# A third of some softmax tiles exponentiated on VectorE, unpadded projections, and a paced background queue

## The chip, the cores and the metric

The kernel runs on one core of a Trainium2 chip. The metric is device time in microseconds (us) of one execution. The engines are named as in the profile: PE (matrix multiply), ACT (activation functions), DVE (vector), POOL (GpSimd) and SP (here only an issuer of DMAs). [...]

## The reference

One transformer block on a sequence of 2048 rows of 512 features, 32 heads of 16, all inputs in bf16:

```python
def _A_ref(x, wqkv, wo):                       # attention
    qkv = (x @ wqkv).reshape(B, S, 3, H, Dh)   # transposed to q, k, v: [B, H, S, 16]
    scores = einsum("bhqd,bhkd->bhqk", q, k) * (Dh ** -0.5)
    o = einsum("bhqk,bhkd->bhqd", softmax(scores), v)
    return o.reshape(B, S, D) @ wo
def _B_ref(x, w_gate, w_up, w_down):           # feed-forward, F = 1792
    return (sigmoid(x @ w_gate) * (x @ w_up)) @ w_down
h  = x + _A_ref(layernorm(x), wqkv, wo)
h2 = h + _B_ref(layernorm(h), w_gate, w_up, w_down)
```

The 32 heads times 2048 times 2048 scores make 134 million exponentials; on 128 partitions that is 2048 blocks of 128 x 512.

## The kernel before

The program has three stages.

**The prologue** (lines 78 to 235) loads x and the weights, normalises x in four chunks of 512 rows (`chunk_ln`), transposes it on PE into `xnT`, projects K and Q of the first four heads and all of V (`v_tile`, 16 tiles of 128 rows), and finds a bound for the softmax shift: the largest squared norm of a key (`kmax_mm`, `kmax_red`, `kmax_fin`) and of each query (`q_shift`). The shift is written as a 17th row beside the 16 rows of Q, against a row of ones beside K, so that the score matmul subtracts it. Heads sit at 32-row steps: the projection weights are copied into zero-padded tiles (`wk_pad`, `wq_pad`), so one projection matmul gives 4 heads in 128 columns of which 64 are used. `wo_pad` is padded in the same way.

**The loop** (lines 462 to 486) goes over 683 tiles. A tile is three blocks (the last has two): a block is 128 keys of one head against 512 queries. The order is query chunk `qc` (4), head group `g` (8 of four heads), key tile `kt` (16), head `j` (4). For each tile PE makes three score matmuls into one of two PSUM tiles `pss` (L403; the four heads use four 32-row strips of the array), ACT exponentiates all 1536 columns in one instruction into `pt` (L471), and PE multiplies by V with a column of ones into `acc` (L431; 17 columns at four 32-column strips). PE's program order is: scores of tile n+1, then `av(...)` for three or six blocks of earlier tiles, then one `step()` of the background queue.

The background queue `bg` holds Python generators that issue everything else a piece at a time: K and Q projections of the other head groups (`prep_k`, `prep_q`), and, for a finished chunk, the output projection and LayerNorm (`wo_ln`) and the feed-forward (`ffn`). Each `yield` ends a tile's share: mostly four matmuls of 128 x 128 x 512, in every tile that has them. All of it goes through one PSUM bank `pm`, which DVE or ACT must read before the next piece may write. When a group's 16 key tiles are done, `finish_group` transposes and divides `acc` on DVE.

**The tail** (lines 488 to 513) does output projection, LayerNorm and feed-forward of the last chunk, with nothing beside it.

Names for the steps: `pss` scores, `pt` exponentials, `acc` sums, `pm` background bank, `th` tanh, `hT` gated product, `sh` the shift row, `kr` and `k` the key maxima.

Of the kernel before, what the change touches and what calls it, by code (L numbers as in the profile page):

```python
# [10 lines left out]
BF16 = mybir.dt.bfloat16  # L11
I32 = mybir.dt.int32
# [3 lines left out]
ENG = mybir.EngineType  # L16


@with_exitstack
def kernel(  # L20
# [18 lines left out]
    NG = H // 4  # L39
    FC = F // P  # L40
# [4 lines left out]
    VW = DH + 1  # L45
    PSUM = bass.MemoryType.PSUM
# [45 lines left out]
    nc.gpsimd.memset(Vaug[:, :, :, DH:DH + 1], 1.0)
    nc.gpsimd.memset(wo_pad[:], 0.0)
    nc.vector.memset(sel[:], 0.0)
    for j in range(4):
        nc.vector.memset(sel[32 * j:32 * j + DH, j:j + 1], 1.0)
    nc.vector.tensor_reduce(out=e16[:], in_=ident_bf[:, DH:P:32], axis=AX.X, op=ALU.add)
    for b in o2buf:
        nc.vector.memset(b[:], 0.0)
    wo_v = A_wo.rearrange("(g j r) n -> j r g n", j=4, r=DH)  # L100
    for j in range(4):
        nc.gpsimd.dma_start(out=wo_pad[32 * j:32 * j + DH, :, :], in_=wo_v[j])
# [4 lines left out]
    def bank0():  # L107
        return ps0.tile([P, 512], FP32, name="b0")

    def ln_stats(src, mv):  # L110
        st = small.tile([P, nc.vector.BN_STATS_DIM], FP32, name="st")
        nc.vector.bn_stats(out=st[:], in_=src)
        nc.vector.bn_aggr(out=mv, in_=st[:])

    def ln_apply(dst, src, mv, rstd):
        nc.vector.tensor_scalar(out=dst, in0=src, scalar1=mv[:, 0:1], scalar2=rstd,  # L116
                                op0=ALU.subtract, op1=ALU.mult)

    def transpose4(ps, src):
        pt = ps[:].bitcast(BF16)[:, 0:DC * P].rearrange("p (b q) -> p b q", b=DC)  # L120
# [362 lines left out]
    while avq:  # L483
        av(GU)
# [59 lines left out]
```

## Time and profile before

| | us |
|---|---|
| median of 6 runs (1169.43 to 1174.78) | 1171.15 |
| the profiled execution, its own time | 1169.7 |
| its span from first to last instruction | 1167.9 |
| first exponential starts | 72.93 |
| last accumulation after the exponentials starts | 1109.60 |

Busy over the span: ACT 84%, PE 80%, DVE 23%, POOL 7%. Busy shares are means over stages: the stretches with background matmuls and those without behave differently, and the granted clock of PE differs between them. In the rows, a time in front is the start or the stretch in us from the span's start; `<-` behind an idle time names what ended it.

### The profile page before, as it was taken

What the parts mean: (1) busy time and instruction counts of PE and PEld (TensorE: products, weight loads), DVE (VectorE), ACT (ScalarE), POOL (GpSimd) and SP (SyncE); (2) the same over time, 40 slices, a digit from 0 to 9 for tenths busy, and PEclk for the clock granted to TensorE, in tenths of its full rate; (3) what the DMA queues carried; (4) which work ended last, traced back from release to release, by engine and by line L of the source; (5) the groups of instructions that cost most, each with busy time, mean ns of one, the idle gap of its engine ahead of it and who ended that gap; (6) DMA issues with size and microseconds to landing.
All of it is one profiled execution on the core that took longest, in us unless ns stands there. A gap on an engine that the chain in (4) does not pass through costs nothing.

```text
span 1167.9 us, 13140 instructions
## 1 busy us (share of the span) xinstructions
PE 937.8 (80%) x5336; PEld 287.6 (25%) x5408; DVE 265.2 (23%) x526; ACT 980.5 (84%) x774; POOL 86.1 (7%) x82
## 2 busy tenths in 40 slices
PE   3668777877887888787787898788788888888878
PEld 1212222222222322222222232222222322222233
DVE  5423323311123211111123212211124211000063
ACT  2359899899987997999987997899988998999911
POOL 6022222200000000000000000100000000000000
PEclk9778899776577998756678999765678998555589
DMA  5000000050000000000000000000000001000000
GB/s 144 1 1 1 1 1 1 1 190 1 1 19 1 1 1 19 2 1 1 1 19 1 1 1 19 1 1 1 1 19 1 1 1 37 1 1 1 1 1 19
DMA packets 11741, 14.87 MB, mean 13 GB/s; under 512 B 928, under 2 KB 10528, under 8 KB 11680
## 3 DMA queue, kind: packets, MB, share of 16 engines
q1 hardware_dynamic: 9904, 11.93, 3.1%
q10 hardware_dynamic: 1584, 1.57, 0.4%
q0 software_dynamic: 192, 0.52, 0.3%
q8 instruction: 42, 0.69, 0.2%
q14 instruction: 19, 0.16, 0.0%
HBM read 11.80 MB, written 2.10 MB: 12 GB/s over the span
## 4 chain that ended last, share of the span: by engine, by line
ACT 39%; PE 32%; issue 16%; DVE 10%; DMA 1%; POOL 0%; SPq 0%; ACTq 0%; DVEq 0%; POOLq 0%
ACT pt L471 37%; PE pm L147 6%; PE pss L403 6%; PE acc L431 5%; PE pm L352 4%; PE pss L502 2%; DVE hT L347 2%; PE pm L309 2%; PE b L201 2%; ACT th L340 1%; DVE xn L116 1%; PE pm L336 1%; DVE KT L156 1%; PE pss L511 1%; PE pm L344 1%
## 5 line engine op out<-in xcount | busy, mean ns | idle before, releaser
L471 ACT ACTIVATE pt<-pss 128x1536 bf16<-128x1536 f32 (+1 forms) x683 | 941.5, 1553 | 83.9 <-PE pss L403 61.6
L403 PE MATMUL pss<-qt,KT 32*128 32x512 bf16 x2048 | 336.8, 481 | 131.0 <-ACT pt L471 119.7
L431 PE MATMUL acc<-pt,Vaug 128*17 128x512 bf16 x2048 | 340.2, 482 | 1.5 <-DVE xs L412 1.0
L403 PEld LDWEIGHTS <-KT 32*128 32x128 bf16 x2048 | 107.2, 94 | 410.5 <-issue 398.0
L431 PEld LDWEIGHTS <-Vaug 128*17 128x17 bf16 x2048 | 66.2, 89 | 222.6 <-issue 222.4
L412 DVE STREAM_TRANSPOSE xs<-acc 128x512 f32<-128x512 f32 x32 | 22.9, 717 | 430.3 <-PE acc L431 429.8
L161 POOL TENSOR_TENSOR sq<-qt 128x512 bf16<-128x512 bf16 x32 | 33.3, 1040 | 678.3 <-DVE qt L187 667.2
L347 DVE SCALAR_TENSOR_TENSOR hT<-th,pm 128x512 bf16<-128x512 f32 x42 | 28.8, 685 | 138.8 <-ACT pt L471 105.1
L336 PE MATMUL pm<-hnT,wg 128*128 128x512 bf16 x147 | 44.2, 395 | 12.6 <-DVE hT L347 10.8
L352 PE MATMUL pm<-wd,hT 128*128 128x512 bf16 x159 | 45.7, 397 | 10.6 <-DVE ob L362 8.6
L147 PE MATMUL pm<-xnT,wq_pad 128*128 128x512 bf16 x102 | 46.2, 543 | 4.8 <-issue 4.2
L344 PE MATMUL pm<-hnT,wu 128*128 128x512 bf16 x168 | 44.2, 386 | 0.0
L161 POOL TENSOR_TENSOR sq<-KT 128x512 bf16<-128x512 bf16 x32 | 33.3, 1041 | 98.8 <-DVE KT L156 57.5
L340 ACT ACTIVATE th<-pm 128x512 f32<-128x512 f32 x42 | 32.4, 773 | 9.3 <-PE pm L336 9.3
L195 DVE TENSOR_SCALAR sh<-pm,kmax 4x512 bf16<-4x512 f32 x31 | 22.9, 739 | 67.5 <-PE acc L431 36.1
L505 ACT ACTIVATE th<-pss 128x512 f32<-128x512 f32 x14 | 8.4, 598 | 35.1 <-PE pss L502 33.9
L147 PE MATMUL pm<-xnT,wk_pad 128*128 128x512 bf16 x105 | 31.6, 415 | 7.1 <-DVE KT L156 6.3
L156 DVE TENSOR_SCALAR KT<-pm,e 128x512 bf16<-128x512 f32 x28 | 21.0, 749 | 38.3 <-PE pm L147 38.3
L309 PE MATMUL pm<-wo_pad,ot 128*128 128x512 bf16 x90 | 25.6, 394 | 4.9 <-DVE h L314 3.6
L122 PE MATMUL b<-ident_bf,xn 128*128 128x128 bf16 x64 | 7.2, 254 | 25.4 <-DVE xn L116 25.4
L187 DVE CAST qt<-pm 128x512 bf16<-128x512 f32 x31 | 20.8, 672 | 24.2 <-PE pm L147 24.2
L336 PEld LDWEIGHTS <-wg 128*128 128x128 bf16 x168 | 15.4, 99 | 32.0 <-issue 22.9
(84 smaller groups left out, 401.6 us busy)
## 6 DMA issues: line engine op xcount, KB each, us to landing
xb<-in_A_x_dram SPq DMA_DIRECT2D x4, 512.0 KB
xr<-in_A_x_dram SPq DMA_DIRECT2D x4, 512.0 KB
out_dram<-ob SPq DMA_DIRECT2D x16, 128.0 KB
wg<-in_B_w_gate_dram SPq DMA_DIRECT2D x1, 1792.0 KB
wu<-in_B_w_up_dram SPq DMA_DIRECT2D x1, 1792.0 KB
wd<-in_B_w_down_dram SPq DMA_DIRECT2D x1, 1792.0 KB
wk_raw<-in_A_wqkv_dram ACTq DMA_DIRECT2D x1, 512.0 KB
wv_sb<-in_A_wqkv_dram ACTq DMA_DIRECT2D x1, 512.0 KB
```

Of the source, the lines that this page charges most:

```text
L147: nc.tensor.matmul(ps[:], lhsT=w_pad[:, d, 4 * g:4 * g + 4, :].rearrange("p h r -> p (h r)"), rhs=xnT[:, d, c * QC:(c + 1) * QC], start=(d ...
L156: nc.vector.tensor_scalar(out=dst, in0=ps[:], scalar1=e16[:, 0:1], scalar2=None, op0=ALU.add)
L161: nc.gpsimd.tensor_tensor(out=sq[:], in0=src, in1=src, op=ALU.mult)
L309: nc.tensor.matmul(ps[:], lhsT=OT[qc, g][:, i * P:(i + 1) * P], rhs=wo_pad[:, g, :], start=(g == 0), stop=(g == NG - 1))
L336: nc.tensor.matmul(ps[:], lhsT=wg[:, d, f * P:(f + 1) * P], rhs=hnT[:, d, :], start=(d == 0), stop=(d == DC - 1))
L340: nc.scalar.activation(out=th[:], in_=ps[:], func=ACT.Tanh, scale=0.5)
L344: nc.tensor.matmul(ps[:], lhsT=wu[:, d, f * P:(f + 1) * P], rhs=hnT[:, d, :], start=(d == 0), stop=(d == DC - 1))
L347: nc.vector.scalar_tensor_tensor(out=hT[:, f, :], in0=th[:], scalar=1.0, in1=ps[:], op0=ALU.add, op1=ALU.mult)
L352: nc.tensor.matmul(ps[:], lhsT=hT[:, f, i * P:(i + 1) * P], rhs=wd[:, f, :], start=(f == 0), stop=(f == FC - 1))
L403: nc.tensor.matmul(pss[:, ui, :], lhsT=KT[g][32 * j:32 * j + 32, kt * P:(kt + 1) * P], rhs=QT[qc, g][32 * j:32 * j + 32, :], start=True, s ...
L431: nc.tensor.matmul(state["acc"][32 * j:32 * j + VW, :], lhsT=Vaug[:, kt, 4 * g + j, :], rhs=pt[:, ui, :], start=(kt == 0), stop=(kt == NT ...
L471: nc.scalar.activation(out=pt[:, 0:w, :], in_=pss[:, 0:w, :], func=ACT.Exp, scale=DH ** -0.5)
```

## The change

It rewrites most of the kernel, with the same mathematics.

1. **Exponentials on DVE.** In 158 of the 683 tiles (counted in the program; about one in four) ACT exponentiates two of the three blocks, and DVE the third, by seven instructions: it scales the score to an integer whose high bits are the exponent of 2 and low 9 bits the fraction, and adds a quadratic correction (`dexp_first`). The program picks the tiles with two counters of planned time, `clock["A"]` for ACT and `clock["D"]` for DVE.
2. **Unpadded projections.** One projection matmul now covers 8 heads (`proj8`); DVE or ACT copies the result to SBUF and eight DMAs of 16 x 512 on SP's queue spread it to the 32-row steps (`spread`). K takes 16 projections in place of 32, Q 16 in place of 32; the output projection takes 4 matmuls per row tile in place of 8. Squares move from POOL to DVE. The shift row goes out on POOL's queue in place of SP's, as do the four small DMAs of `kr`.
3. **Pacing.** V sums are issued in even tiles, up to 8 at a time; background matmuls in odd tiles, at most 4; results are read out at the earliest one tile later.
4. **Prologue and tail.** Eight of the 16 V tiles move into the loop; statistics of chunk c+1 are issued ahead of the transposes of chunk c; normalising moves from DVE to POOL and ACT; POOL fills `QT` and `KT` of groups 4 to 7 in between; the key maxima stay on their partitions (no DMA in the prologue). In the tail, three of the four output projection matmuls of each row tile stand ahead of the last V sums.

The core of the diff:

```diff
-        nc.scalar.activation(out=pt[:, 0:w, :], in_=pss[:, 0:w, :], func=ACT.Exp,
-                             scale=DH ** -0.5)
-        av(GU if len(avq) <= 2 * GU else 2 * GU)
-        for ui, u in enumerate(group):
-            avq.append((u, pt, ui))
-        step()
+        pend = sum(c[0] for c in chain)
+        split = (w == GU and last_kt < NT - 4 and not chain
+                 and clock["D"] + pend <= clock["A"] + 0)
+        wa = w - 1 if split else w
+        eins = nc.scalar.activation(out=pt[:, 0:wa, :], in_=pss[:, 0:wa, :], func=ACT.Exp, scale=SC)
+        clock["A"] += 98 + 427 * wa
+        if split:
+            jins = dexp_first(pss[:, GU - 1, :], uns[-1])
+            tc.declare_no_dep(jins.ins, eins.ins, reason="two readers of different banks")
+        avq.extend(uns)
+        run_chain(clock["A"] - 400)
+        if n % 2 == 0:
+            av(8)
+            run_bg(0)
+        else:
+            run_bg(4)
+        run_chain(clock["A"] + 600)
+        clock["D"] = max(clock["D"], clock["A"] - 600)
...
+    def dexp_first(src, un):
+        J = dvx.tile([P, QC], U16, name="J", bufs=2)
+        dv(720)
+        jins = nc.vector.tensor_scalar(out=J[:], in0=src, scalar1=512 * SC * LOG2E, scalar2=512 * 127.0,
+                                op0=ALU.mult, op1=ALU.add)
...
+        chain.extend([
+            (210, lambda: V.tensor_scalar(out=a[:], in0=J[:], scalar1=511, scalar2=None,
+                                          op0=ALU.bitwise_and)),
+            (320, lambda: V.tensor_scalar(out=b[:], in0=J[:], scalar1=0xFE00, scalar2=None,
+                                          op0=ALU.bitwise_or)),
+            (460, lambda: V.tensor_tensor(out=b[:].bitcast(BF16), in0=a[:],
+                                          in1=b[:].bitcast(I16), op=ALU.mult)),
+            (330, lambda: V.tensor_scalar(out=a[:].bitcast(BF16), in0=a[:],
...
+            (460, lambda: V.tensor_tensor(out=a[:].bitcast(BF16), in0=a[:].bitcast(BF16),
+                                          in1=b[:].bitcast(BF16), op=ALU.mult)),
+            (690, lambda: V.scalar_tensor_tensor(out=r[:], in0=J[:], scalar=0.25,
...
+    def run_chain(limit):
+        while chain and clock["D"] < limit:
+            ns, f = chain.popleft()
+            dv(ns)
+            f()
...
+    def spread(dst_pair, src, cols):
+        for a in range(2):
+            for j in range(4):
+                r = (4 * a + j) * DH
+                nc.sync.dma_start(out=dst_pair[a][32 * j:32 * j + DH, cols], in_=src[r:r + DH, :])
...
-        nc.sync.dma_start(out=QT[qc, g][DH:P:32, :], in_=sh[:])
+        for a in range(2):
+            nc.gpsimd.dma_start(out=QT[2 * p + a][DH:P:32, :], in_=sh[4 * a:4 * a + 4, :])
...
+    c_stats(0)
+    xns = c_apply(0)
+    for c in range(NQC):
+        if c + 1 < NQC:
+            c_stats(c + 1)
+        c_trans(c, xns)
+        if c + 1 < NQC:
+            xns = c_apply(c + 1)
+        if c == 0:
+            fill(range(4, NG))
...
+        c_proj(c)
...
+    wide = [ps_s.tile([P, GU, QC], FP32, name="pss") for _ in range(2)]
+    hps = [wide[i % 2][:, i // 2, :] for i in range(TQ)]
+    for i in range(TQ):
+        wo_mm(hps[i], qc, i, 0, NP - 1)
     while avq:
-        av(GU)
+        st["n"] += 1
+        av(64)
```

How this moves the instructions, at three places. First PE in the feed-forward (matmuls only, `wg` and `wu` are the gate and up weights). Before:

```order
L403 MATMUL pss_4999<-qt_3802,KT1_81 128x512
L431 MATMUL acc_507<-pt_4973,Vaug_88 17x512
...
L431 MATMUL acc_507<-pt_4988,Vaug_88 17x512
L336 MATMUL pm_5010<-hnT_4776,wg_1994 128x512
...
L403 MATMUL pss_5015<-qt_3802,KT1_81 128x512
...
L431 MATMUL acc_507<-pt_5003,Vaug_88 17x512
L403 MATMUL pss_5026<-qt_3802,KT1_81 128x512
...
L431 MATMUL acc_507<-pt_5019,Vaug_88 17x512
L344 MATMUL pm_5035<-hnT_4776,wu_1996 128x512
```

Now, in the first feed-forward (`xnT0` is reused for the transposed input, `dr` holds a block that DVE made):

```order
L532 MATMUL pss_3765<-QT2_93,KT2_85 128x512
...
L584 MATMUL acc_528<-dr_3729,Vaug_99 17x512
L584 MATMUL acc_528<-pt_3742,Vaug_99 17x512
...
L584 MATMUL acc_528<-pt_3758,Vaug_99 17x512
...
L532 MATMUL pss_3787<-QT2_93,KT2_85 128x512
...
L422 MATMUL pm_3794<-xnT0_79,wg_1708 128x512
...
L532 MATMUL pss_3801<-QT2_93,KT2_85 128x512
```

Three V sums stood between the scores of every two tiles; now seven stand in one gap and the four gate matmuls alone in the next. The gate and up pieces were three tiles' worth for one of the 14 columns of F; they are now four.

Second, DVE late in the last chunk, where nothing of the background is left. Before, these rows are the end of one chunk's output and two finished groups:

```order
L420 STREAM_TRANSPOSE ot_7700<-o2_0_99 128x512
L362 SCALAR_TENSOR_TENSOR ob_7702<-pm_7646,h_6835 128x512
...
L362 SCALAR_TENSOR_TENSOR ob_7864<-pm_7813,h_6835 128x512
L412 STREAM_TRANSPOSE xs_7955<-acc_507 128x512
L414 RECIPROCAL rec_7957<-xs_7955 128x16
L417 TENSOR_TENSOR o2_1_100<-xs_7955,rec_7957 128x16x16
```

Now, behind a finished group there (one whole block of exponentials, `J` to `dr`, and the start of the next):

```order
L549 STREAM_TRANSPOSE xs_10081<-acc_528 128x512
L551 RECIPROCAL rec_10083<-xs_10081 128x16
L554 TENSOR_TENSOR o2_1_107<-xs_10081,rec_10083 128x16x16
L595 TENSOR_SCALAR J_10112<-pss_10092 128x512
L603 TENSOR_SCALAR da_10114<-J_10112 128x512
L605 TENSOR_SCALAR db_10115<-J_10112 128x512
L607 TENSOR_TENSOR db_10115<-da_10114,db_10115 128x512
L609 TENSOR_SCALAR da_10114<-da_10114 128x512
L613 TENSOR_TENSOR da_10114<-da_10114,db_10115 128x512
L615 SCALAR_TENSOR_TENSOR dr_10116<-J_10112,da_10114 128x512
L595 TENSOR_SCALAR J_10146<-pss_10134 128x512
```

DVE had four instructions per group there; it now has seven more for each split tile, back to back.

Third, PE at the end of the loop (`ot` are the finished groups of the last chunk). Before:

```order
L431 MATMUL acc_507<-pt_8718,Vaug_88 17x512
...
L431 MATMUL acc_507<-pt_8723,Vaug_88 17x512
...
L309 MATMUL pss_8744<-wo_pad_90,ot_7127 128x512
L309 MATMUL pss_8744<-wo_pad_90,ot_7415 128x512
...
L309 MATMUL pss_8744<-wo_pad_90,ot_8737 128x512
```

Now:

```order
L584 MATMUL acc_528<-pt_10297,Vaug_99 17x512
L368 MATMUL pss_10307<-wo_sb_101,ot_8653 128x512
L368 MATMUL pss_10307<-wo_sb_101,ot_9277 128x512
L368 MATMUL pss_10307<-wo_sb_101,ot_9824 128x512
L368 MATMUL pss_10308<-wo_sb_101,ot_8653 128x512
...
L584 MATMUL acc_528<-pt_10299,Vaug_99 17x512
...
L368 MATMUL pss_10307<-wo_sb_101,ot_10332 128x512
```

Twelve output projection matmuls now stand between the last scores' sums and the last two V sums.

## Rows read from the trace of the kernel before

**Rows 1.** The page, part 1: busy us of each engine, share, instructions.
```profile
PE 937.8 (80%) x5336; PEld 287.6 (25%) x5408; DVE 265.2 (23%) x526; ACT 980.5 (84%) x774; POOL 86.1 (7%) x82
```
**Rows 2.** L471 by stretch: stretch, its us, ACT busy (instructions), granted clock, DMA share, GB/s.
```profile
72.00:240.00 168.00, 147.93 (x108) 0.88 0.00 1
240.00:337.00 97.00, 93.08 (x70) 0.61 0.16 58
337.00:477.00 140.00, 120.42 (x86) 0.93 0.03 8
...
866.00:985.00 119.00, 104.46 (x74) 0.96 0.03 9
```
**Rows 3.** Stretches, all engines: PE, PEld, DVE, ACT, POOL busy; then as above.
```profile
985.00:1110.00 125.00, 105.94 (x559) 27.36 (x556) 8.43 (x16) 124.53 (x93) 0.00 (x0) 0.52 0.02 6
72.00:1110.00 1038.00, 855.24 (x4974) 251.15 (x5039) 208.65 (x394) 951.61 (x725) 61.38 (x59) 0.76 0.03 10
```
**Rows 4.** By line and shape, 985 to 1110: count | busy us, mean ns | idle.
```profile
L471 ACT ACTIVATE pt<-pss 128x1536 bf16<-128x1536 f32 x92 | 124.0, 1610 | 0.0
```
**Rows 5.** The same for the whole span: busy us, mean ns, idle before, releasers.
```profile
L471 ACT ACTIVATE pt<-pss 128x1536 bf16<-128x1536 f32 x682 | 940.6, 1554 | 83.9 <-PE pss L403 61.6 <-PE acc L431 22.1
L347 DVE SCALAR_TENSOR_TENSOR hT<-th,pm 128x512 bf16<-128x512 f32 x42 | 28.8, 685 | 138.8 <-ACT pt L471 105.1 <-PE pm L344 33.8
L156 DVE TENSOR_SCALAR KT<-pm,e 128x512 bf16<-128x512 f32 x28 | 21.0, 749 | 38.3 <-PE pm L147 38.3
L505 ACT ACTIVATE th<-pss 128x512 f32<-128x512 f32 x14 | 8.4, 598 | 35.1 <-PE pss L502 33.9 <-remote 1.1
```
**Rows 6.** Timeline (start, us, engine, line), first background matmuls, lower clock.
```profile
76.14 1.89 PE L147 MATMUL pm<-xnT,wk_pad 128*128 128x512 bf16 x4
...
80.33 1.45 ACT L471 ACTIVATE pt<-pss 128x1536 bf16<-128x1536 f32 x1 [0.47 <-PE pss L403]
```
**Rows 7.** One line: ns min/median/max, first and last start, form.
```profile
L116 DVE TENSOR_SCALAR xn<-xb,mv,rstd x16: 394/405/4307, 9.7 to 54.1; 128x512 bf16<-128x512 bf16 x16
```
**Rows 8.** Timeline in the first feed-forward, upper clock.
```profile
400.69 1.04 PE L344 MATMUL pm<-hnT,wu 128*128 128x512 bf16 x4
...
401.88 0.39 PE L403 MATMUL pss<-qt,KT 32*128 32x512 bf16 x3 [0.15 <-ACT pt L471]
...
402.20 0.39 PE L431 MATMUL acc<-pt,Vaug 128*17 128x512 bf16 x3
...
405.04 0.60 PE L431 MATMUL acc<-pt,Vaug 128*17 128x512 bf16 x6
```
**Rows 9.** Timeline in the last chunk, lower clock.
```profile
1041.40 0.61 PE L403 MATMUL pss<-qt,KT 32*128 32x512 bf16 x3 [0.20 <-ACT pt L471]
1041.95 0.60 PE L431 MATMUL acc<-pt,Vaug 128*17 128x512 bf16 x3
```
**Rows 10.** Timeline of the prologue.
```profile
9.66 4.31 DVE L116 TENSOR_SCALAR xn<-xb,mv,rstd 128x512 bf16<-128x512 bf16 x1
10.01 3.81 POOL L93 MEMSET wo_pad<- 128x4096 bf16 x1
...
33.61 5.32 PE L201 MATMUL b<-wv_sb,xnT 128*128 128x512 bf16 x16
...
65.53 2.63 SPq L174 DMA_DIRECT2D k<-kr  x4
...
69.33 0.14 DVE L178 TENSOR_REDUCE kmax<-k 4x1 f32<-4x4 f32 x1 [3.83 <-DMA k<-kr]
...
72.28 1.03 PE L403 MATMUL pss<-qt,KT 32*128 32x512 bf16 x6 [7.50 <-DMA qt<-sh]
72.93 4.24 ACT L471 ACTIVATE pt<-pss 128x1536 bf16<-128x1536 f32 x3 [8.18 <-PE pss L403]
```
**Rows 11.** DMA issues by line, median us from issue to landing.
```profile
wo_pad<-in_A_wo_dram POOLq DMA_DIRECT2D x4, 128.0 KB, 4.2
```
**Rows 12.** Timeline at the end of the loop.
```profile
1109.60 0.60 PE L431 MATMUL acc<-pt,Vaug 128*17 128x512 bf16 x2 [0.31 <-ACT pt L471]
```

More of the change, by code (lines that the diff above doesn't have):

```diff
@@ L39 @@
     NG = H // 4
+    NP = NG // 2
     FC = F // P
@@ L97 @@
[L97 to L102, printed above, removed]
-    ps0ctx = ExitStack()
-    ps0 = ps0ctx.enter_context(tc.tile_pool(name="ps0", bufs=8, space=PSUM))
-    def bank0():
-        return ps0.tile([P, 512], FP32, name="b0")
+    nc.vector.memset(sel[:], 0.0)
@@ new lines, in c_trans, with c_proj @@
+    def c_trans(c, xns):
+        for i in range(TQ):
+            pt = transpose4(bank0(), xns[i])
+            dst = xnT[c][:, :, i * P:(i + 1) * P]
+            if i % 2:
+                nc.scalar.copy(out=dst, in_=pt)
+            else:
+                nc.vector.tensor_copy(out=dst, in_=pt)
+    def c_proj(c):
+        pk = bank0()
+        proj8(pk, wk_sb, 0, c)
+        kd = work.tile([P, QC], BF16, name="kd", bufs=4)
+        nc.scalar.copy(out=kd[:], in_=pk)
+        spread(KT[0:2], kd, slice(c * QC, (c + 1) * QC))
+        sq = square(kd)
@@ new lines @@
+    xns = c_apply(0)
[7 more added lines that the diff above has]
+            fill(range(4, NG))
+        if c == NQC - 1:
+            pq = bank0()
+            nc.tensor.matmul(pq[0:8, :], lhsT=sel[:, 0:8], rhs=cst["sqq"][:], start=True, stop=True)
+            nc.scalar.activation(out=small.tile([P, 1], FP32, name="warm")[:], in_=eps_t[:],
+                                 func=ACT.Exp)
+        c_proj(c)
@@ L235 @@
+    k_fin(k4, 0)
+    q_shift(pq, 0)
+    for a in range(2):
+        for j in range(4):
+            r = 32 * j + DH * a
+            nc.gpsimd.dma_start(out=wo_sb[r:r + DH, :, :], in_=wo_v[a, j])
     ps0ctx.close()
@@ L393, with scores @@
     units = [(qc, g, kt, j) for qc in range(NQC) for g in range(NG)
              for kt in range(NT) for j in range(4)]
-    groups = [units[i:i + GU] for i in range(0, len(units), GU)]
-    state = {"acc": acc_init, "n2": 0, "qc_open": 0}
-    avq = deque()
-    def scores(group):
+    tiles = [units[i:i + GU] for i in range(0, len(units), GU)]
+    def scores(tl):
         pss = ps_s.tile([P, GU, QC], FP32, name="pss")
-        for ui, (qc, g, kt, j) in enumerate(group):
-            force(("q", qc, g))
+        for ui, (qc, g, kt, j) in enumerate(tl):
+            force(("q", qc, g // 2))
@@ new lines, in av @@
+    def av(limit):
+        if st["defer"]:
+            st["defer"] = False
+        i = 0
+        while i < len(avq) and limit:
+            un = avq[i]
+            qc, g, kt, j = un.u
+            if qc * NG + g != st["cur"]:
+                return
+            if un.ready is None or un.ready >= st["n"]:
+                i += 1
+                continue
+            force(("v", kt))
+            avq.pop(i)
+            limit -= 1
+            c = count.get((qc, g, j), 0)
+            count[qc, g, j] = c + 1
+            nc.tensor.matmul(acc[32 * j:32 * j + VW, :], lhsT=Vaug[:, kt, 4 * g + j, :],
+                             rhs=un.ap, start=(c == 0), stop=(c == NT - 1),
```

619 lines of the change are left out of this document (358 added, 261 removed).

## The prediction

> **What bounds the kernel now.** Read the page first [rows 1]: ACT is busy 84% of the span and PE 80%, so neither bounds all of it. Then the table by stage [rows 2, 3], which separates two kinds of stretch in the loop. Without background matmuls (four stretches, 469 us, 338 exponentials; the first and the last stand in the rows) PE is granted 0.52 to 0.61 of its clock and ACT hardly waits: in the last one it is busy 124.53 of 125 us, PE 105.94 [rows 3]. There, 92 instructions in 124.0 us [rows 4] make 1.348 us a tile; that is ACT's own pace. With background matmuls (the feed-forward, three stretches, 401 us, 244 exponentials; and the K and Q projections, 168 us, 108 exponentials) the grant is 0.88 to 0.96 and ACT waits. Last, the groups of the whole span [rows 5] say for whom: 83.9 us of idle time ahead of the exponentials, 61.6 of it ended by the score matmuls.
>
> So the loop, from the first exponential at 72.93 [rows 10] to the last V sums at 1109.60 [rows 12], 1036.7 us, is ACT's work plus waits. Its work is 683 x 1.348 = 921 us and 42 tanh: one alone takes 0.598 [rows 5], and some 0.1 of that hides behind a neighbour, as 1.45 alone [rows 6] against 1.348 in a row shows for the large one; 42 x 0.5 = 21. Together 942; 95 us are lost. By stage, stretch less exponentials x 1.348 less tanh: 168 - 146 = 22 in the projections, 401 - 329 - 21 = 51 in the feed-forward, 469 - 456 = 13 in the rest; the borders of the stages are the remainder.
>
> **The change, part by part.**
>
> *ACT's work.* 512 columns cost (1.45 - 0.598) / 2 = 0.426 us. 158 tiles lose one block: 158 x 0.426 = 67 us. New work: 942 - 67 = 875 us.
>
> *DVE's new work.* Seven instructions a split tile, none of which stands in the trace. The first reads PSUM: 0.749 as L156; the last has three operands: 0.685 as L347 [rows 5]. Three have one SBUF input: 0.405 is the median of L116 [rows 7], the upper bound; half of it, 0.20, is my lower one. Two have two SBUF inputs: between 0.41 and 0.69, the same two rows. The sum is 2.85 to 4.05 us. The program plans 3.19; since its 720 and 690 ns for the first and the last lie within 5% of the rows, I take 3.3. 158 x 3.3 = 521 us beside about 200 us that DVE has in the loop already (208.65 [rows 3]; fewer transposes, more squares): 721 of some 940 us. Even the upper end, 840, is covered by ACT's own time, so DVE's total is no limit; lateness of single results can be (a rival).
>
> *PE in the loop.* Every two tiles have two score groups, one batch of about six V sums and, where there is background, four matmuls. At the upper clock: scores 0.32 (401.88 to 402.20), six sums 0.60, four matmuls 0.96 of their 1.04 before the next group starts [rows 8]: 2 x 0.32 + 0.60 + 0.96 = 2.2 us. At the lower: scores 0.55 (1041.40 to 1041.95 [rows 9]), four matmuls 1.82 of their 1.89 [rows 6], so 0.45 each; six sums are two rounds of that and a hand-over, 1.0: 3.9 us. ACT needs 2 x 1.348, less 0.426 in about every second pair, plus half a tanh in the feed-forward: 2.74 us. PE is under it at the upper clock and over it at the lower. Before, a tile with a gate piece had 0.32 + 0.32 + 0.96 = 1.6 us against 1.348, so PE was late there even at the upper clock; paced, it isn't.
>
> *What stays lost.* By the program's order 68 tiles stand beside projections, 312 beside the feed-forward and its LayerNorm, 303 beside neither. Projections: 0.2 us a tile as before, 14 us. Feed-forward: a mean grant of 0.93 is the lower clock for a seventh of the time; in some 16 of 156 pairs PE takes 3.9 and not 2.74, 18 us, and 7 for hand-overs. Rest, at the lower clock: PE needs 2 x 0.55 + 1.0 = 2.1 a pair and ACT at least 2.27, but the batch of sums stands whole ahead of one score group, so pairs with a split tile lose about 0.15: 70 x 0.15 = 10, and 13 as now. Sum 62; it could be 30 (no hand-over late) or 110 (as now, and 15 more). Loop: 875 + 62 = 937 us, 100 less than 1036.7.
>
> *Prologue.* Removed: two chunks' V tiles, 16 matmuls in up to 5.32 us [rows 10], about 10 us; the key maxima's way over DMA, 65.53 to 69.33 [rows 10], 3.8 us; the first normalising, 4.31 us where the median is 0.405 [rows 7, 10] while POOL filled `wo_pad`, 3.9 us. Added: DVE fills two `KT` of 2048 columns ahead of its first statistics, some 2 us late; the shift row goes by POOL, whose DMA took 4.2 us to land [rows 11], where finishing the maxima, the shift and SP's DMA together took 2.95 (69.33 to 72.28): 2 us more. The eight spreading DMAs of the last chunk are issued beside that. Net some 15 us less: the first exponential at 58. At best 50, if statistics ahead of the transposes also hide the LayerNorm wait of about 2 us in each chunk. At worst 66: POOL's new fills (four `KT`, four `QT`; by the pace of L93, 3.81 us for 4096 columns [rows 10], together 9 us) stand in the middle of the prologue, and L116 shows that a DVE instruction can wait for such a fill.
>
> [...] L116 was a one-input form; beside the fills now stand squares, with two inputs. [...]
>
> *Tail.* 58.3 us now lie behind 1109.60 [rows 12]. Nine of the twelve output projections set ahead of the last two V sums need the last exponential's PSUM tile; at 0.45 us each they hold these sums up by 4 us, and the division of the last group behind them. The projections that are already made and the transposes half copied by ACT give some 2 back: 60 us.
>
> Sum: 58 + 937 + 60 = 1055 us of span; with the 1.8 us around it (1169.7 - 1167.9) 1057. The median of the runs lies 1.4 us above the profiled one: **1058 us**, 9.7% under 1171.15.
>
> **The rivals.**
>
> *PE at the lower clock where the background runs (slower).* Stretches without background are granted 0.52 to 0.61 though PE is busy 85% in the last of them [rows 2, 3]. The change thins the feed-forward from 2.6 to 2.1 background matmuls a tile, counted in the program. If its grant falls to the lower level, 190 pairs (projections too) at 3.9 in place of 2.74 add 220 us, less the 32 counted already: 1246. It decides where 66% of the pairs run so, a mean grant of about 0.63 there: below it the kernel is slower than before. Against it: in time the thinning is small, 1.6 to 1.5 a microsecond, as the tiles get shorter; and the projection stretch had 1.1 at a grant of 0.88. Chance 4%. A grant of 0.8, a third of the pairs, adds some 50 us: 1110; 11%.
>
> *The DVE blocks come late.* PE's order is fixed, so a V sum on a block that isn't there yet holds up the next scores. If the chain takes 4.05 and not the planned 3.19, each is 0.86 us late; PE's slack of about 0.3 a pair leaves 0.5: 158 x 0.5 = 80 us, 1138. For it: five of the seven instructions have only bounds. Against it: the first and the last agree with the rows, and DVE has a fifth of its time free to catch up. 12%.
>
> *ACT hardly waits.* Loop 875 + 20, prologue 50, tail 58, 2 around: 1005. For it: at the upper clock PE has half a microsecond to spare in each pair. Against it: `acc` is single, and a new group's first sums wait for DVE to read it. 12%.
>
> **How the numbers follow.** The forecast has 61%, with a range of its own from 1020 to 1100 (30 to 95 us lost, prologue 50 to 66). The range for 8 in 10 is 995 to 1130: it takes in the case without waits and the grant of 0.8, and leaves out most of the late blocks and the lower clock. A measurement of this kernel tells about 0.2% from no change. Slower is the first rival, 4%, and 1% from the others' far ends; within 0.2% has 1%; faster 94%.
>
> **What would show it.** Right: a two-block exponential starts the next one 0.92 us later; ACT loses near 60 us in the loop, most of it to scores; a grant near 0.9 in the feed-forward; DVE's seven instructions near 3.3 us; the first exponential at 58. Wrong: PE waiting for `dr` ahead of V sums (late blocks); a grant under 0.8 in the feed-forward (the first rival); squares stretched over POOL's fills (a prologue of 66).

## The result and the profile after

The changed kernel takes **1049.37 us** (median of 8 runs, 1045.79 to 1050.09) against 1169.99 for the kernel before on the same chip: a ratio of 0.896, 95% interval 0.8945 to 0.8973. The forecast was 1058 us. The profiled execution took 1046.45 us with a span of 1044.7; before it was 1169.7 and 1167.9. Of the run with the shift rows on SP's queue, below, one execution in four took 2935.81 us and is left out of its median.

The page's first part answers to [rows 1]:

```profile
PE 822.4 (79%) x5121; PEld 227.9 (22%) x5184; DVE 688.3 (66%) x1583; ACT 911.0 (87%) x777; POOL 60.9 (6%) x79
```

DVE's busy time rises from 265 to 688 us, ACT's falls from 980 to 911. The stretches of the loop (stretch, its us, ACT busy and its instructions, granted clock, DMA share, GB/s) answer to [rows 2]; projections come first, then stretches without background and with the feed-forward take turns:

```profile
55.60:154.00 98.40, 90.62 (x71) 0.87 0.10 25
154.00:283.00 129.00, 127.40 (x102) 0.55 0.14 48
283.00:442.00 159.00, 144.31 (x125) 0.90 0.03 8
442.00:525.00 83.00, 80.96 (x65) 0.61 0.03 7
525.00:686.00 161.00, 154.30 (x134) 0.97 0.04 10
686.00:757.00 71.00, 69.51 (x56) 0.57 0.02 4
757.00:908.00 151.00, 141.21 (x122) 0.94 0.03 10
908.00:980.00 72.00, 71.36 (x58) 0.50 0.00 1
```

The granted clock stands as a share of PE's full speed. Of the 924 whole microseconds from 56 to 980, 378 were granted 0.50 and 501 were granted 1.00, the others something between. In this document 0.50 is the lower clock and 1.00 the upper.

The second column less the third of the table is what ACT loses: 7.8 us in the projections, 31.2 in the three feed-forward stretches (14.7, 6.7, 9.8), 5.7 in the rest; 44.7 in all. By line and shape (count | busy us, mean ns | idle before, releasers), beside [rows 5]:

```profile
L654 ACT ACTIVATE pt<-pss 128x1536 bf16<-128x1536 f32 x524 | 746.2, 1543 | 39.3 <-PE pss L532 38.2
...
L654 ACT ACTIVATE pt<-pss 128x1024 bf16<-128x1024 f32 x159 | 179.2, 1127 | 8.0 <-PE pss L532 7.7
L615 DVE SCALAR_TENSOR_TENSOR dr<-J,da 128x512 uint16<-128x512 uint16 x158 | 109.0, 690 | 4.9
L595 DVE TENSOR_SCALAR J<-pss 128x512 uint16<-128x512 f32 x158 | 108.5, 687 | 171.9 <-PE pss L532 171.3
...
L584 PE MATMUL acc<-dr,Vaug 128*17 128x512 bf16 x158 | 74.0, 469 | 0.2 <-DVE dr L615 0.2
L613 DVE TENSOR_TENSOR da<-da,db 128x512 bf16<-128x512 bf16 x158 | 67.2, 425 | 5.3
L607 DVE TENSOR_TENSOR db<-da,db 128x512 bf16<-128x512 uint16 x158 | 66.6, 421 | 4.2
L603 DVE TENSOR_SCALAR da<-J 128x512 uint16<-128x512 uint16 x158 | 46.4, 294 | 5.1
L609 DVE TENSOR_SCALAR da<-da 128x512 bf16<-128x512 uint16 x158 | 46.4, 293 | 5.3
L605 DVE TENSOR_SCALAR db<-J 128x512 uint16<-128x512 uint16 x158 | 45.1, 285 | 0.0
```

ACT's wait ahead of exponentials falls from 83.9 to 47.3 us (39.3 and 8.0). DVE's chain is 3.10 us (the means' sum), and PE waited 0.2 us for it in the whole program.

Where the 123.2 us between the spans went: the first exponential starts at 55.59 in place of 72.93 [rows 10], 17.3 us; from there to the last V sums (984.38 now, 1109.60 before [rows 12]) it is 928.8 in place of 1036.7, 107.9 us; behind them 60.3 in place of 58.3, 2.0 us back.

### The profile page after: what moved, and what is told of

The parts are those of the page before. It is cut to its first block, busy times and chain, and to the rows that moved or that the text cites. A ratio compares the mean times of both kernels' runs of the same rounds, so it can differ in the third digit from the quotient of the medians.

```text
span 1044.7 us, 14125 instructions
## 1 busy us (share of the span) xinstructions
PE 822.4 (79%) x5121; PEld 227.9 (22%) x5184; DVE 688.3 (66%) x1583; ACT 911.0 (87%) x777; POOL 60.9 (6%) x79
## 4 chain that ended last, share of the span: by engine, by line
ACT 46%; PE 21%; issue 19%; DVE 11%; DMA 1%; POOL 1%; another core or an unknown queue 0%; SPq 0%; ACTq 0%; DVEq 0%; POOLq 0%
ACT pt L654 44%; PE pss L532 5%; PE acc L584 3%; PE pss L422 3%; PE pm L422 2%; PE pm L134 2%; ACT th L445 1%; DVE st L122 1%; PE pm L368 1%; PE pm L432 1%; DVE J L595 1%; DVE hT L427 1%; PE pss L432 1%; DVE h L384 1%; PE b L171 1%
## 5 line engine op out<-in xcount | busy, mean ns | idle before, releaser
L654 ACT ACTIVATE pt<-pss 128x1536 bf16<-128x1536 f32 (+1 forms) x683 | 871.0, 1446 | 47.3 <-PE pss L532 45.9
L532 PE MATMUL pss<-QT,KT 32*128 32x512 bf16 x2048 | 329.1, 471 | 128.5 <-ACT pt L654 116.8
L584 PE MATMUL acc<-pt,Vaug 128*17 128x512 bf16 x1890 | 272.5, 478 | 0.1
L595 DVE TENSOR_SCALAR J<-pss 128x512 uint16<-128x512 f32 x158 | 108.5, 687 | 171.9 <-PE pss L532 171.3
L615 DVE SCALAR_TENSOR_TENSOR dr<-J,da 128x512 uint16<-128x512 uint16 x158 | 109.0, 690 | 4.9
L584 PE MATMUL acc<-dr,Vaug 128*17 128x512 bf16 x158 | 74.0, 469 | 0.2 <-DVE dr L615 0.2
L613 DVE TENSOR_TENSOR da<-da,db 128x512 bf16<-128x512 bf16 x158 | 67.2, 425 | 5.3
L607 DVE TENSOR_TENSOR db<-da,db 128x512 bf16<-128x512 uint16 x158 | 66.6, 421 | 4.2
L609 DVE TENSOR_SCALAR da<-da 128x512 bf16<-128x512 uint16 x158 | 46.4, 293 | 5.3
L603 DVE TENSOR_SCALAR da<-J 128x512 uint16<-128x512 uint16 x158 | 46.4, 294 | 5.1
L427 DVE SCALAR_TENSOR_TENSOR hT<-th,pm 128x512 bf16<-128x512 f32 x42 | 28.5, 680 | 25.4 <-PE pm L422 21.2
## 6 DMA issues: line engine op xcount, KB each, us to landing
wd<-in_B_w_down_dram SPq DMA_DIRECT2D x1, 1792.0 KB, 17.3
```

What stands on the lines that cost most here:

```text
L532: nc.tensor.matmul(pss[:, ui, :], lhsT=KT[g][32 * j:32 * j + 32, kt * P:(kt + 1) * P], rhs=QT[g][32 * j:32 * j + 32, :], start=True, stop= ...
L584: nc.tensor.matmul(acc[32 * j:32 * j + VW, :], lhsT=Vaug[:, kt, 4 * g + j, :], rhs=un.ap, start=(c == 0), stop=(c == NT - 1), tile_positio ...
L595: jins = nc.vector.tensor_scalar(out=J[:], in0=src, scalar1=512 * SC * LOG2E, scalar2=512 * 127.0, op0=ALU.mult, op1=ALU.add)
L603: (210, lambda: V.tensor_scalar(out=a[:], in0=J[:], scalar1=511, scalar2=None, op0=ALU.bitwise_and)),
L607: (460, lambda: V.tensor_tensor(out=b[:].bitcast(BF16), in0=a[:], in1=b[:].bitcast(I16), op=ALU.mult)),
L609: (330, lambda: V.tensor_scalar(out=a[:].bitcast(BF16), in0=a[:], scalar1=EXP_C1 / (512 * 512 * 4), scalar2=EXP_C0 / (512 * 4), op0=ALU.mu ...
```

## Experiments

Each edit is on the changed kernel. A ratio is to the kernel before, with its 95% interval.

**No block on DVE.**

```diff
-        split = (w == GU and last_kt < NT - 4 and not chain
+        split = (False and w == GU and last_kt < NT - 4 and not chain
```

> The changed kernel, but no block goes to DVE: all 683 exponentials are ACT's, whole (1536 columns, 11 of them 1024). Everything else of the change stays (V tiles unpadded, background paced by pairs of tiles, prologue, tail). Theory A (ACT's work is the bound, and each DVE block takes 0.426 us from it): 158 x 0.426 = 67 us come back, less what of the 47 us that ACT still waits is caused by the shorter tiles, 10 to 20: 1095 to 1116 us against 1049, still 55 to 75 under the kernel before. Rival R (pacing and the thinner PE work made the gain, DVE's blocks only hide behind waits): within 10 us of 1049. ACT's idle time ahead of the exponentials: A 25 to 47 us, R 90 or more.

Measured: 1094.56 us, 0.9352 (0.9337 to 0.9368). From the page, part 1 and the exponentials' group of part 5:

```profile
PE 823.7 (75%) x5121; PEld 227.7 (21%) x5184; DVE 230.3 (21%) x477; ACT 973.2 (89%) x777; POOL 60.7 (6%) x79
...
L654 ACT ACTIVATE pt<-pss 128x1536 bf16<-128x1536 f32 (+1 forms) x683 | 933.8, 1633 | 33.9 <-PE pss L532 30.0
```

DVE's blocks are worth 45 us: theory A, 0.4 us under its range. (682 of the exponentials have 1536 columns and one has 1024, not 11.) ACT's busy time is 62 us longer without them (973.2 against 911.0; 67 were priced), and its wait 13 us shorter: 49, as the spans differ (1093.4, 1044.7). The rival that the blocks only fill waits is refuted, and so is the thought that they are most of the gain: 76 us stand without them. Of the spans' 74.5, 18.4 are prologue (its first exponential is at 54.55) and 50 the exponentials' wait (83.9 to 33.9). No run takes the unpadded projections out alone.

**The order of before inside the loop.**

```diff
-        if n % 2 == 0:
-            av(8)
-            run_bg(0)
-        else:
-            run_bg(4)
+        av(GU if len(avq) <= 4 * GU else 2 * GU)
+        run_bg(4)
```

> The changed kernel, but with the order of before inside the loop: after each tile's scores three or six V sums and then one step of the background, in place of eight sums after an even tile and the background after an odd one. DVE's blocks stay (the planner then places 150 instead of 158, 3 us by ACT's count). Theory A (a tile with sums and a background piece takes PE longer than ACT's tile even at the upper clock, and only pairs let ACT's second PSUM tile cover it): ACT waits 20 to 40 us more beside the feed-forward, 1070 to 1090 us. Rival R2 (the order within a pair costs nothing, PE catches up in the next tile): 1049 to 1054.

Measured: 1130.91 us, 0.9667 (0.9636 to 0.9698), 82 us more; the direction of A at over twice its size. The timeline of PE in a feed-forward:

```profile
633.21 0.39 PE L532 MATMUL pss<-QT,KT 32*128 32x512 bf16 x3
...
634.13 1.02 PE L422 MATMUL pm<-xnT,wg 128*128 128x512 bf16 x4 [0.20 <-DVE hT L427]
635.09 0.39 PE L532 MATMUL pss<-QT,KT 32*128 32x512 bf16 x3
```

From one score group to the next PE needs 1.88 us at the upper clock (granted 1.00), against 1.35 of ACT. The exponentials' group in the page:

```profile
L654 ACT ACTIVATE pt<-pss 128x1536 bf16<-128x1536 f32 (+1 forms) x683 | 873.1, 1389 | 108.3 <-PE pss L532 93.6 <-PE acc L584 11.8
```

Waits rise by 61 us here and by 9 ahead of tanh. Of the remaining 12, the eight blocks that DVE has fewer (150) are 3; the rest I put down to overlap between ACT's instructions that a wait breaks up (1.45 alone, 1.35 in a row), which no run isolates. The clock isn't the cause: from 610 to 660 us of this run PE was granted 1.00 and ACT was busy 42.29 of the 50 us.

**Thin background, but sums with every tile.**

```diff
-        if n % 2 == 0:
-            av(8)
-            run_bg(0)
-        else:
-            run_bg(4)
+        av(GU if len(avq) <= 4 * GU else 2 * GU)
+        run_bg(0 if n % 2 == 0 else 4)
```

> Between the changed kernel and the run whose order was that of before (sums and background in each tile, 1131 us): the background comes only every second tile, as in the changed kernel, but three or six V sums follow each tile's scores, as before. It tells which half of the pacing made the 82 us. Theory D (density: a tile with a gate piece takes PE 1.6 to 1.8 us and ACT waits; every second tile without one gives PE the time back): 1049 to 1065. Rival B (batches: 1898 + 150 sums took PE 448 us in threes and 347 us in the changed kernel's batches, since a round of three costs as much as one of four and each round a hand-over to the scores; that is what was lost): 1100 or more.

Measured: 1042.31 us, 0.8912 (0.8889 to 0.8934): theory D, 7 us below its range. Against the run with the order of before only the pace of the background differs, and it makes 89 us (4 of them nine blocks more on DVE, 159 for 150): density is all of it. The batches of up to eight sums give nothing (this run is even 7 us faster than the changed kernel), although PE's busy time on sums does fall with them (334.8 + 74.0 us here, 272.5 + 74.0 in the changed kernel). That PE time was hidden.

**187 blocks on DVE.**

```diff
-                 and clock["D"] + pend <= clock["A"] + 0)
+                 and clock["D"] + pend <= clock["A"] + 2500)
-        run_chain(clock["A"] - 400)
+        run_chain(clock["A"] + 600)
-        run_chain(clock["A"] + 600)
+        run_chain(clock["A"] + 2500)
```

> The changed kernel with 187 blocks on DVE instead of 158 (the planner lets DVE run later against ACT). Theory A (ACT's work is the bound, DVE has a third of its time free and its results are early enough): 29 x 0.426 = 12 us less, 1035 to 1042. Rival L (DVE's results become the late ones, since the more blocks the shorter their lead): the wait for DVE's block ahead of the V sums, 0.2 us in the changed kernel, grows to 15 us or more and the time is 1049 or above. Rival P (PE, busy 79% and at the lower clock without background, becomes the bound): no wait for DVE, but ACT's waits for scores grow by the 12 us, and the time stays within 3 us of 1049.

Measured: 1065.48 us, 0.9102 (0.9089 to 0.9116). The time is rival L's, but the wait is at another place than L said. PE's waits (line, for whom: us, times, longest):

```profile
PE pss L532 <- DVE J L595: 18.2, 27, 1.9
...
PE acc L584 <- DVE dr L615: 5.4, 10, 1.3
```

The end of the chain is 5.4 us late, its beginning 18.2: `J` is DVE's only reading of the PSUM tile, and the next scores may not overwrite it until then. In the changed kernel that wait is 1.0 us. The edit also moves the chain's instructions in DVE's order (the two limits of `run_chain`), so the 16 us are not shown to be the price of the 29 blocks alone.

**A longer chain that the planner doesn't know of.** The `db` instruction of 0.285 us stands four times in place of once (the added lines three times over).

```diff
             (320, lambda: V.tensor_scalar(out=b[:], in0=J[:], scalar1=0xFE00, scalar2=None,
                                           op0=ALU.bitwise_or)),
+            (0, lambda: V.tensor_scalar(out=b[:], in0=J[:], scalar1=0xFE00, scalar2=None,
+                                        op0=ALU.bitwise_or)),
```

> The changed kernel with one of the chain's seven DVE instructions issued three times more in each of the 158 chains, which the planner doesn't know of: by the trace 3 x 0.285 = 0.86 us more a chain, 3.95 us instead of 3.10, 135 us more DVE work. It measures the price of late blocks by itself. The prediction's price (each of 158 chains 0.86 us late, PE's slack takes 0.3 of it): 80 us more, 1130. Theory S (the blocks have a lead of more than a microsecond over their V sums, and DVE has 30% of its time free): 0 to 20 us more, 1049 to 1070, with DVE busy near 820 us.

Measured: 1134.27 us, 0.9684 (0.9638 to 0.9729), 85 us more; theory S falls. The waits:

```profile
PE pm L422 <- DVE hT L427: 37.2, 23, 2.6
PE acc L584 <- DVE dr L621: 31.8, 36, 1.9
```

The prediction's price for late blocks (80 us) is about what it costs, but not by its sum, in which each of the 158 sums waits half a microsecond: only 36 waits of V sums for blocks stand here, 31.8 us (0.2 in the changed kernel), and the feed-forward waits 37.2 us (8.8 there) for DVE's product of gate and up, which stands in the same queue. What kept that rival away, I take it, is that the planned 3.19 us cover the measured 3.10; no run lengthens the chain and the plan together.

**The tail, the chunk ends, the prologue, each alone.** First the last sums ahead of the twelve partial projections:

```diff
-    for i in range(TQ):
-        wo_mm(hps[i], qc, i, 0, NP - 1)
     while avq:
         st["n"] += 1
         av(64)
+    for i in range(TQ):
+        wo_mm(hps[i], qc, i, 0, NP - 1)
```

> The changed kernel, but behind the loop the last V sums are issued ahead of the twelve partial output projections, as before the change. The prediction priced the change's order at 4 us (nine projections wait for the last exponential's PSUM tile and hold two V sums up, and the last group's division behind them). Theory A: the sums run 3.9 us earlier (984.4 becomes 980.5 us in the changed kernel's trace), the projections fill the division's time, and the kernel is 2 to 4 us faster, 1045 to 1047. Rival T (the division and DVE's work behind it are not what ends last in the tail, or the projections are then late): within 1 us of 1049.

Measured: 1045.25 us, 0.8915 (0.8892 to 0.8938). The timeline of ACT with the last exponentials and the first copy in the tail, of the changed kernel:

```profile
934.21 46.55 ACT L654 ACTIVATE pt<-pss 128x1536 bf16<-128x1536 f32 x37 [0.51 <-PE pss L532]
999.69 0.59 ACT L702 COPY xnT<-pss 128x512 bf16<-128x512 bf16 x1 [18.93 <-PE pss L128]
```

and of this one:

```profile
936.68 46.56 ACT L654 ACTIVATE pt<-pss 128x1536 bf16<-128x1536 f32 x37 [0.51 <-PE pss L532]
999.79 0.59 ACT L702 COPY xnT<-pss 128x512 bf16<-128x512 bf16 x1 [16.55 <-PE pss L128]
```

From the last exponential to the copy it is 16.55 us in place of 18.93: 2.4 of the priced 4 us come back. The medians differ by 4.1 us, the spans (1044.2, 1044.7) by 0.5 only, as the last exponential ends 2.5 us later in this execution (983.24, 980.76).

Then the output projection and LayerNorm at the chunk ends, where the loop passes from one query chunk to the next:

```diff
-        xr = load_xr(qc, 0)
+        xrs_ = [load_xr(qc, 0), load_xr(qc, 1)]
+        for _ in range(4):
+            yield "wait"
...
-            h_out(ps, h, mv, i, xr)
-            xr = nxt
+            h_out(ps, h, mv, i, xrs_[i])
+            if i + 2 < TQ:
+                xrs_.append(load_xr(qc, i + 2))
+            yield "wait"
+            yield "wait"
         rstd = small.tile([P, TQ], FP32, name="rstd")
         rstd_newton(rstd[:], mv[:, :, 1])
+        dv(1700)
+        for _ in range(4):
+            yield "wait"
         for i in range(TQ):
-            yield "wait"
             hn = hn_apply(h, mv, rstd, i)
+            yield "wait"
+            yield "wait"
             yield 2
```

> The changed kernel, but the output projection and LayerNorm between two chunks are spread over more tiles: two residual rows are loaded ahead, two tiles lie between a row's projection and the next, four more behind the Newton steps for 1/sqrt (planned 1.3 us, measured 3.0), and two between normalising a row and its transposes; the planner counts 1.7 us more for the Newton steps. Theory A (ACT's waits that are left sit at the three chunk ends, where PE stands for DVE's h and normalised rows, some 20 of 47 us): 10 to 20 us less, 1030 to 1040. Rival W (PE's other background work takes their place, or the waits move to where the feed-forward now ends, closer to the next chunk end): within 4 us of 1049.

Measured: 1030.84 us, 0.8807 (0.8789 to 0.8826). What stood there in the changed kernel, at its last chunk end:

```profile
761.16 1.86 PE L368 MATMUL pm<-wo_sb,ot 128*128 128x512 bf16 x4 [3.14 <-DVE h L384]
...
763.67 7.74 ACT L654 ACTIVATE pt<-pss 128x1536 bf16<-128x1536 f32 x6 [3.41 <-PE pss L532]
...
773.80 0.61 PE L128 MATMUL pm<-ident_bf,hn 128*128 128x128 bf16 x4 [4.62 <-DVE hn L390]
...
775.06 10.58 ACT L654 ACTIVATE pt<-pss 128x1536 bf16<-128x1536 f32 x8 [3.65 <-PE pss L532]
```

PE's queue holds the next scores behind matmuls that wait for DVE, and ACT pays both times. With the edit ACT's wait for scores falls from 45.9 to 30.7 us, and the span by 15.6:

```profile
L662 ACT ACTIVATE pt<-pss 128x1536 bf16<-128x1536 f32 (+1 forms) x683 | 868.4, 1439 | 31.5 <-PE pss L540 30.7
```

And the prologue:

```diff
-                nc.gpsimd.tensor_scalar(out=xn[:], in0=xb[c][:, i, :], scalar1=mv[:, i, 0:1],
+                eng = nc.vector if c == 0 else nc.gpsimd
+                eng.tensor_scalar(out=xn[:], in0=xb[c][:, i, :], scalar1=mv[:, i, 0:1],
...
             cst["sqq"] = square(qd)
+        if c + 2 < NQC:
+            c_stats(c + 2)
...
-        if c + 1 < NQC:
-            c_stats(c + 1)
         c_trans(c, xns)
+        if c == 0:
+            c_stats(1)
...
-        if c == 0:
-            fill(range(4, NG))
+        if c < 3:
+            fill(((4,), (5,), (6, 7))[c])
```

> The changed kernel with another order in the prologue: the first chunk's two rows that POOL normalised in 2.07 us each go to DVE, the LayerNorm statistics of a chunk stand on DVE behind the squares of the chunk two before it, no longer ahead of the copies of the transposes of the chunk just before, and POOL's fills are spread over three chunks. By the changed kernel's trace the K projections of the second and third chunk wait 4.38 us each for such a copy, and the first transposes 2 us for POOL. Theory A: two waits gone and the first chunk 2 us earlier, the first exponential at 45 to 50 us (55.6) and 1040 to 1044. Rival S (the chunk's own chain, from its statistics over POOL's 4.1 us to the transposes, is as long; PE then waits for the normalised rows instead): 53 to 56 us, and the time unchanged.

Measured: 1039.39 us, 0.8874 (0.8853 to 0.8894). The first exponential starts at 49.27, in place of 55.59, in the timeline:

```profile
49.27 3.71 ACT L657 ACTIVATE pt<-pss 128x1024 bf16<-128x1024 f32 x3 [5.71 <-PE pss L535]
```

The 6.3 us answer to the spans (1044.7, 1038.8: 5.9). The medians differ by 10; single runs of the changed kernel alone lie between 1045.79 and 1050.09, so I hold to the spans. The edit changes three things at once; PE's waits tell two of them apart: its first one, for normalised rows, falls from 12.4 to 10.7 us, and the two of 4.38 for the copies, 8.8 together, are gone but for 0.7.

**The shift rows from SP's queue.**

```diff
-            nc.gpsimd.dma_start(out=QT[2 * p + a][DH:P:32, :], in_=sh[4 * a:4 * a + 4, :])
+            nc.sync.dma_start(out=QT[2 * p + a][DH:P:32, :], in_=sh[4 * a:4 * a + 4, :])
```

> The changed kernel, but the shift rows (the two small DMAs behind the key maxima) are issued by SP as before, not by POOL. The prediction counted 2 us for POOL's way in the prologue; the changed kernel's trace has 2.0 us from POOL's issue (52.90) to the first scores (54.91). Theory A: SP's way is within 1 us of that in the prologue, and beside the loop the shift is not waited for: 1046 to 1051, no difference to 1049. Rival Q: SP's queue holds the spreading DMAs, eight for each projection, and the shift behind them comes late in the loop: PE waits for the shift rows there, 1055 or more.

Measured: 1060.05 us (median of three), 0.9052 (0.9037 to 0.9068): rival Q. SP's queue in the loop:

```profile
124.94 6.27 SPq L141 DMA_DIRECT2D KT<-kd  x10
131.31 4.96 SPq L141 DMA_DIRECT2D QT<-qd  x8
136.37 1.12 SPq L167 DMA_DIRECT2D QT<-sh  x2
```

and who waits behind it, in the timeline of the other engines:

```profile
138.74 0.74 DVE L164 TENSOR_SCALAR sh<-pm,kcol 8x512 bf16<-8x512 f32 x1 [8.46 <-DMA QT<-sh]
...
139.54 0.58 PE L134 MATMUL pm<-xnT,wk_sb 128*128 128x512 bf16 x1 [8.40 <-DVE sh L164]
```

Eighteen spreading DMAs of 0.62 us each on SP stand ahead of the two shift rows, DVE can't overwrite the one `sh` buffer, and PE waits for DVE. In the whole loop ACT's wait for scores rises from 45.9 to 60.9 us.

**Together.** The three edits:

> Three edits together: the last V sums ahead of the partial output projections (alone 1045.25), the output projection and LayerNorm spread over more tiles (alone 1030.84), the prologue's order (alone 1039.39). Theory A (three different stretches of one chain, so the gains add: 4.1 + 18.5 + 10.0 = 33 us): 1014 to 1021. Rival V (they overlap, or a chunk end moved against the clock gives some back): 1025 or more.

Measured: 1022.46 us, 0.8735 (0.8724 to 0.8747), 1 us above A's range. In medians 27 of 33 us add; in spans all do (0.5 + 15.6 + 5.9 = 22.0 priced, 23.8 measured, 1020.9). With the sums of every tile:

> The three edits together, and V sums with every tile instead of every second (alone 1042.31 with 159 blocks on DVE; here 156). Theory A: 4 to 7 us below the three edits alone, 1008 to 1016. Rival V (the 7 us came from chunk ends that the three edits have already thinned, and threes of sums cost PE more): the same as the three edits alone or up to 5 us above.

Measured: 1024.45 us, 0.8753 (0.8726 to 0.8781): by the medians V, no gain. But the six executions lie between 1016.84 and 1029.52, and the profiled one is the fastest: its span is 1015.0, 5.9 us under the three edits' 1020.9, as A has it. Which of the two holds stays open. Finally, on top of these four:

```diff
-                 and clock["D"] + pend <= clock["A"] + 0)
+                 and clock["D"] + pend <= clock["A"] + 600)
```

> The run before (three edits, V sums with every tile) with 172 blocks on DVE instead of 156, by a planner that lets DVE be 0.6 us behind ACT. By ACT's count 16 x 0.426 = 7 us less. But 187 blocks in the changed kernel made it 16 us slower, since the scores waited for DVE to read its block. Theory L (the planner's balance has no slack, its block is read late whenever DVE starts behind ACT): the same or up to 10 us slower. Rival A2 (the lead is there until some 170 blocks): 5 to 8 us faster.

Measured: **1016.67 us**, 0.8689 (0.8676 to 0.8701): by the medians 7.8 us less, by the spans (1013.7, 1015.0) 1.3. The size is open between A2 and L; L's cause is not there, since PE's wait for `J` stays at 1.2 us (1.0 in the run before). The exponentials' busy time falls by 5.8 us (869.0 to 863.2), and ACT's wait ahead of them rises by 2.3 (32.3 to 34.6). It is the fastest version, 3% under the changed kernel; of its four executions the slowest took 1018.96, and the fastest of the three edits alone 1022.08.

## Why the prediction was right

The forecast span was 1055 us and 1044.7 came. The prologue is 2.4 us under its term, the waits in the loop 17 (44.7 for 62); ACT's work is 5 over (880 for 875), 3.6 of held sums stand in the loop and not in the tail, and the tail is 0.3 over. The mechanism is right; in several terms, named below, errors cancel.

*ACT is the bound, and its work 875 us: right.* The loop's 928.8 us less 44.7 of waits and 3.6 of held sums at the end is 880. In the run with the order of before, single instructions of both widths stand alone in the timeline:

```profile
637.28 1.02 ACT L654 ACTIVATE pt<-pss 128x1024 bf16<-128x1024 f32 x1 [0.16 <-PE pss L532]
...
639.27 1.45 ACT L654 ACTIVATE pt<-pss 128x1536 bf16<-128x1536 f32 x1
```

512 columns cost 0.43 us, as priced (0.426). The sign named for it came too: a two-block exponential with another instruction right behind it starts that one 0.90 us later in the changed kernel's trace (0.92).

*DVE's chain 3.3 us, total no limit: right by 0.2 us, and too comfortable.* The three one-input instructions took 0.29, between the two bounds (0.20, 0.405). The conclusion that DVE has a fifth of its time free holds for the total only: 135 us of unplanned work cost 85, and 29 blocks more, issued by a looser plan, 16.

*What stays lost, 62 us: 44.7.* Projections 7.8 for 14, feed-forward 31.2 for 25, rest 5.7 for 23. The feed-forward's size is near, its cause was wrong: that term came out by luck. I gave 18 us to pairs at the lower clock, and read a mean grant of 0.93 as a seventh of the time at 0.50 and the rest at 1.00 (before, 971 of the 1037 whole microseconds from 73 to 1110 were granted one or the other); but ACT's waits between 285 and 320, 525 and 560, 757 and 800 us add up to 21.7, and these are chunk ends where PE stands for DVE's `h` and normalised rows. The chunk-end run shows it. In the rest, "pairs with a split tile lose about 0.15" did not happen: 1.6, 2.0, 1.5 and 0.6 us in stretches with 281 exponentials.

*Pacing.* "Before, PE was late there even at the upper clock; paced, it isn't": shown by the two order runs. Taken out of the changed kernel alone, it is worth 82 us, DVE's blocks 45; what either would give without the other was not run. It is the number of background matmuls per tile that counts, not the batches.

*Prologue 58: 55.59, with errors that cancel.* The terms add up to 13.7 us (17.7 removed, 4 added) and were rounded up to 15; 17.3 came. The squares (0.42, within 2 ns for all 32) were not stretched, as the timeline of the prologue shows:

```profile
18.69 0.42 DVE L152 TENSOR_TENSOR sq<-kd 128x512 bf16<-128x512 bf16 x1 [3.16 <-ACT kd L234]
18.93 1.79 POOL L109 MEMSET KT<- 128x2048 bf16 x1
...
20.50 0.42 DVE L152 TENSOR_TENSOR sq<-qd 128x512 bf16<-128x512 bf16 x1
```

The first square ends 0.18 us after a fill has begun, the second begins 0.22 us before that fill ends. By this the 66 is out, which took L116's wait beside a fill over to the squares; that they would be spared no trace had shown, as none had one beside a fill. The step "2 us more" for the shift by POOL was too large: from finishing the maxima to the first scores it is 3.41 us (51.50 to 54.91), for 2.95 before. The timeline of the changed kernel:

```profile
51.50 0.14 DVE L157 TENSOR_REDUCE kcol<-k4a 8x1 f32<-8x4 f32 x1
...
52.90 1.31 POOL L167 DMA_DIRECT2D QT<-sh  x2 [7.60 <-DVE sh L164]
...
54.91 1.04 PE L532 MATMUL pss<-QT,KT 32*128 32x512 bf16 x6 [4.15 <-DMA QT<-sh]
```

With SP's queue in the changed kernel (the run above) the issue and the scores come 2.1 and 1.8 us later, so there POOL's way is the shorter one:

```profile
54.99 1.19 SPq L167 DMA_DIRECT2D QT<-sh  x2
...
56.73 1.03 PE L532 MATMUL pss<-QT,KT 32*128 32x512 bf16 x6 [5.92 <-DMA QT<-sh]
```

*Statistics ahead of the transposes* were taken as a possible gain that hides the LayerNorm waits. With the new split of the normalising that gain is there: behind its first wait PE stood 11.4 us for normalised rows before (25.4 less 14.0) and 1.0 now (13.4 less 12.4). But a cost came with it that the sum lacks: the K projections of two chunks waited 4.38 us each for the copies behind the statistics, and the prologue run took that out.

*Tail 60: 60.3, by luck.* The sums are held as described and start 3.6 us behind the last exponential's end at 980.76 (0.31 before [rows 12]), and 2.4 us of it are on the path. But this stretch lies ahead of the last sums, in the loop's 928.8; the 60.3 are without it. From the last exponential's end to the end of the span it is 63.9 us, for 58.6 before: 5.3 more where the sum has 2. The "2 back" did not come. The timeline there:

```profile
981.26 3.19 PE L368 MATMUL pss<-wo_sb,ot 128*128 128x512 bf16 x10 [0.22 <-issue]
984.38 0.39 PE L584 MATMUL acc<-pt,Vaug 128*17 128x512 bf16 x2
```

*The rivals.* Lower clock in the feed-forward: granted 0.90, 0.97 and 0.94; refuted. Late blocks: 0.2 us; it did not happen. Its price came near in the longer chain's run, half of it by another way. ACT hardly waits: 45 us, and the three edits bring the exponentials' idle time from 47.3 to 30.9.

## What to carry over

Where one engine in program order feeds the bound engine, thin the side work until each pair of steps fits under the bound engine's pace: here, each taken out alone, that was worth more than the work moved off the bound engine. An engine with a third of its time free may still have no slack: read when its first read of a shared buffer comes, not its busy share. Then look at what stands in the feeding queue where stages meet; short chains on another engine (15 instructions of 0.17 us, planned at 1.3 us and 3.0 long) stop everything there.

## What the hardware showed

POOL normalises 128 x 512 in 2.07 us (2.06 to 2.08 in all eight) where DVE took 0.394 to 0.405 [rows 7] and ACT 0.81. Two squares of DVE (their two inputs are the same tile) lie in the second of two such instructions of POOL, which read SBUF. The one at 31.84 began 1.15 us behind the start of POOL's second (30.69), the one at 44.37 stands alike; both took 0.42:

```profile
28.64 4.13 POOL L214 TENSOR_SCALAR xn<-xb,mv,rstd 128x512 bf16<-128x512 bf16 x2 [1.27 <-DMA QT<-qd]
...
31.84 0.42 DVE L152 TENSOR_TENSOR sq<-kd 128x512 bf16<-128x512 bf16 x1 [2.60 <-ACT kd L234]
```

The four runs with the prologue's new order show another case. There a square starts 0.07 us behind POOL's second instruction, and one of the two takes longer. In the last run it is the square, 0.97 us in place of 0.42:

```profile
18.67 2.06 POOL L215 TENSOR_SCALAR xn<-xb,mv,rstd 128x512 bf16<-128x512 bf16 x1
18.74 0.97 DVE L152 TENSOR_TENSOR sq<-kd 128x512 bf16<-128x512 bf16 x1 [2.05 <-ACT kd L235]
```

In the other three POOL's instruction takes 2.31 us, and the square 0.45 or 0.46. What lies between 0.07 and 1.15 us was not run.

PE was granted 0.50 of its clock from 908 to 980 us although it was busy 59.95 of the 72 us, with scores and V sums alone; from 757 to 908, with the feed-forward's matmuls among them, it was busy 119.95 of 151 us and granted 0.94.
